# Top-32 attention and a squared-ReLU layer on one core: last score columns in a bank of their own, and identity products in TensorE's free places

## The chip, the core and the metric

The kernel runs on one core of one Trainium2 chip. Its engines are named as in the profile: PE (TensorE's products; PEld is its loading of weights), DVE (VectorE), ACT (ScalarE), POOL (GpSimd) and SP (SyncE, whose queue SPq starts transfers). The metric is the device time of one launch in microseconds (us); lower is better.

## What is computed

For each of 8 batches and 8 heads there are 576 queries, keys and values of 64 numbers. Of each query's 576 scores only those at or above its 32nd largest enter a softmax. The result, put together as 4608 rows of 512, goes through two matrix products with a squared ReLU between them.

```python
scores = scale * np.matmul(q, k.transpose(0, 1, 3, 2))          # (8, 8, 576, 576)
kth = np.partition(scores, -top_k, axis=-1)[..., -top_k:-top_k + 1]   # top_k = 32
scores = np.where(scores >= kth, scores, -1e9)
attn = np.exp(scores - np.max(scores, axis=-1, keepdims=True))
x = np.matmul(attn / (np.sum(attn, axis=-1, keepdims=True) + 1e-09), v)
...
h = x @ w_in                                # (4608, 512) x (512, 2048)
r = np.maximum(h, 0.0)
return (r * r) @ w_out                      # (2048, 512)
```

## The kernel before

**Unit of work.** A *pair* is 128 queries of two neighbouring heads (block 0 and block 1), 2 x 576 scores on 128 partitions. There are 144 pairs, 18 to a batch. The last 64 queries of four heads make a pair of another shape (`Z`), two to a batch.

**Steps of a pair.** PE makes the scores in three banks of PSUM (`scores`, tile `ps`, float32, 64 rows of the array for each head). ACT copies all 1152 columns to `s`. DVE and POOL find each row's 32nd largest value: an elementwise maximum `m` of the two halves of a row (DVE, which reads one half from PSUM and the other from `s`), a reduction `f` to quarters, sums and differences on POOL, and then MAX8 and MATCH_REPLACE8 in turns until `kth`. ACT makes a mask `w`; PE transposes `s` and adds the mask (`flip`: nine float32 transposes and nine bfloat16 products with `steep_bf`, in two parts of 4 and 5); ACT takes the exponential `p`; PE multiplies by the values (`vb`); ACT copies the result (`av`); DVE takes the reciprocal of the sums (`rzall`), POOL multiplies, PE transposes to `xt`. When a chunk of up to 512 rows is full, `feed` runs the layer: products with `win`, ReLU on ACT, squares, products with `wo`, and a store. This is called the layer below; a batch's layer runs while later pairs are in their attention.

**Buffers in PSUM.** The scores have one set of three banks, the transposed scores another (`ps_e`), and all else that PE writes takes turns in two single banks (`psum`).

**The scores before.** Block 0 lies at columns 0 to 575, block 1 at 576 to 1151. So block 0's last 64 columns share a bank with block 1's first 448, and the two heads use different rows of the array. They are written in two operations: the first makes block 0's 512 columns and all of block 1, the second makes block 0's last 64 and waits for the first by a semaphore; the order puts other work of PE between them where there is some.

**Order.** A planner lists every operation with an engine, an assumed duration, a priority and its inputs, plays the list through (`Plan.schedule`) and so fixes each engine's order, written out with semaphores. On the chip every engine follows that order strictly. `nbf` is the earliest time for an operation, and `lag` moves a chunk's layer to a lower priority.

Of the kernel before, what the change touches and what calls it, by code (L numbers as in the profile page):

```python
# [5 lines left out]
ALU = mybir.AluOpType  # L6
# [70 lines left out]
class Op:  # L77
    __slots__ = ("eng", "dur", "prio", "fn", "deps", "tiles", "takes", "n", "users", "start", "end",
                 "idx", "sem", "val", "ndma", "seq", "vc", "waits", "wars", "later", "nbf", "lk")
# [5 lines left out]
class Plan:  # L85
# [3 lines left out]
    def op(self, eng, dur, prio, fn, r=(), w=(), u=(), hold=(), take=(), after=(), order=(), sem=None, ndma=0, nbf=0.0, lk=False):  # L89

        o = Op()
        o.eng, o.dur, o.prio, o.fn = eng, dur - (.05 if eng == "act" else 0), prio, fn
        o.sem, o.ndma, o.seq, o.nbf, o.lk = sem, ndma, len(self.ops), nbf, lk
        o.takes = list(take)
        o.users = []
        o.start = o.end = o.idx = o.val = o.vc = None
        deps = set(after)
        for t in r:  # L100
            deps.update(t.writers)
        for t in u:
            deps.update(t.ops)
        for t in list(r) + list(w) + list(u) + list(hold):
            t.ops.append(o)
            t.left += 1
        for t in list(w) + list(u):
            t.writers.append(o)
        for t in o.takes:
            t.taker = o  # L110
        o.later = ({t.taker for t in list(r) + list(w) + list(u) + list(hold)} | set(order)) - deps - {o, None}
        o.deps = deps
        o.wars = list(w) + list(u)
        o.tiles = list(r) + list(w) + list(u) + list(hold)
        self.ops.append(o)
        return o

    def schedule(self, t0=0.0, latency=0.12, own=0.07):
# [24 lines left out]
        while events:  # L143
            t = events[0][0]
            while events and events[0][0] <= t + 1e-9:
                _, _, kind, x = heapq.heappop(events)
                if kind == "end":
                    done += 1
                    for tl in x.tiles:
                        tl.left -= 1  # L150
                        if tl.left == 0 and tl.slot is not None:
                            for i in range(tl.width):
                                tl.pool.last[tl.slot + i] = tl
                            tl.pool.give(tl.slot, tl.width)
                    for v in x.users:
                        left[v] -= 1
                        lat = (own if x.eng != "pe" else .25) if v.eng == x.eng else latency
                        readyat[v] = max(readyat[v], t + lat)
                        if left[v] == 0:
                            push(readyat[v], "ready", v)  # L160
                elif kind == "ready":
                    heapq.heappush(ready[x.eng], (x.prio, x.seq, x))
# [45 lines left out]
class Emitter:  # L208
# [59 lines left out]

    def emit(self, plan, e, eng):
        for o in plan.order[e]:  # L270
            for k, v in o.waits:
# [9 lines left out]
def bass_top_k_attn__then__act_relu_squared_kernel(  # L281
# [32 lines left out]
    STEP = 3.2  # L314

# [90 lines left out]

    def mm(o, l, r, start, stop=True):
# [5 lines left out]
    def build(full, weights, pl):  # L413
        state = {"n": 0, "u": 0, "last": {}}
# [6 lines left out]
        def load_pair(b, hp, base):  # L421
            rq, rk, rv = tile("rq"), tile("rk"), tile("rv")

            def load(t, src):
                def fn():
                    r = at(t)
                    res = [nc.sync.dma_start(r[:, 0:4, h, :], src[b, 2 * hp + h, 0:512, :].rearrange(
                        "(tb p) d -> p tb d", p=P)) for h in range(2)]
                    res.append(nc.sync.dma_start(
# [14 lines left out]
            pl.op("sp", 2.3, base - 79.9, load(rk, k), w=[rk], take=[rk], sem=slot_sem, ndma=3)  # L444
# [16 lines left out]
            o_q = pl.op("pe", .55, base - 45, t4(tq, rq), r=[rq], w=[tq], take=[tq, qk])  # L461
            pl.op("pe", .55, base - 44.9, t4(tk, rk), r=[rk], w=[tk], take=[tk], order=[o_q])
# [5 lines left out]
            pl.op("gp", .9, base + 5, lambda: gp.tensor_copy(at(vb)[:, :, 0:D], at(rv)[:, :, :]),  # L468
# [3 lines left out]
        def top_k(gi, qks, tg):  # L472
# [10 lines left out]
            def scores(part):  # L483
# [7 lines left out]
            def scores_z(part):  # L491
                o = wide(ss)
                for i, to, c0, n_, first in PIECES[part]:
                    x = at(qks[i])
                    for h in range(2):
                        ins = mm(o[64 * h:64 * h + 64, to:to + n_], x[64 * h:64 * h + 64, 0, 512:576],
                                 x[64 * h:64 * h + 64, 1, c0:c0 + n_], first)
                return ins

            fs = scores if gi != Z else scores_z  # L500
            qu = sorted(set(qks), key=lambda t: t.num)
            o_s = pl.op("pe", 1.2, tg - LEAD, lambda: fs(0), r=qu, w=[ss], take=[ss, st])
            pl.op("pe", .15, tg - LEAD, lambda: fs(1), r=qu, w=[ss], after=[o_s])
            cp = pl.op("act", 1.15, tg - LEAD + 1, lambda: act.copy(  # L504
                at(st)[:, :, :].rearrange("p i c -> p (i c)"), wide(ss)), r=[ss], w=[st])
# [44 lines left out]
            else:  # L550
# [3 lines left out]
                def whole(dur, prio, op, o, x, y, **kw):  # L554
# [3 lines left out]
                dve(.7, lambda: vec.tensor_tensor(  # L558
                    at(m)[:, :, :], wide(ss).rearrange("p (i c) -> p i c", i=2)[:, :, 0:HALF],
                    at(st)[:, :, HALF:S], ALU.max), dp=-ME, r=[ss], hold=[st], after=[cp], w=[m], take=[m])  # L560
                whole(1.45, tg, ALU.add, lambda: at(t1)[:, :, :], lambda: at(st)[:, :, 0:HALF],
# [4 lines left out]
                whole(.87, tg - MP, ALU.add, lambda: at(t2)[:, :, :], lambda: at(m)[:, :, 0:QUART],  # L566
                      lambda: at(m)[:, :, QUART:HALF], r=[m], w=[t2], take=[t2])
                mid = whole(.87, tg - MP, ALU.subtract, lambda: at(f)[:, :, QUART:HALF], lambda: at(t2)[:, :, :],
                            lambda: at(f)[:, :, 0:QUART], r=[t2], hold=[f], after=[big])
                low = whole(1.45, tg + 2, ALU.subtract, lambda: at(f)[:, :, HALF:S], lambda: at(t1)[:, :, :],  # L570
# [38 lines left out]
        def attend(gi, st, wt, tt):  # L609
# [14 lines left out]
            o_t = pl.op("pe", .75, tt, lambda: flip([0, 128, 256, 384], 0), r=[st, wt], w=[e], take=[e, pt])  # L624
            pl.op("pe", .95, tt + .1, lambda: flip([640, 768, 896, 1024, 512], 4), r=[st, wt], w=[e], order=[o_t])
# [4 lines left out]
        def collect(gi, groups, parts, hp, tt):  # L630
# [19 lines left out]
            pl.op("pe", .2 * nu, tt + 2, lambda: [fav(j, pt, vbs) for j, (pt, vbs) in enumerate(groups)][-1],  # L650
# [3 lines left out]
            rz = pl.op("dve", .1, tt + 4, lambda: vec.reciprocal(rzall[:, r0:r0 + nu], at(avs)[:, 0:nu, 64]), r=[avs])  # L654
            rzs.append(rz)
            pl.op("gp", .15 + .13 * nu, tt + 4, lambda: gp.tensor_tensor(  # L656
# [29 lines left out]
        def feed(chunk, xt, tm, step):  # L686
# [5 lines left out]
            lag = 0 if last else LAG  # L692
            gs = [tile("g") for _ in range(NFB // kf)]
            for i, g in enumerate(gs):
# [15 lines left out]
                ho = pl.op("pe", kf * 4 * (nt / 2200 + .01), tf + lag, fh, r=[xt], w=[hh], take=[hh, g], after=weights,  # L710
# [11 lines left out]
            for tb in range((nt + 127) // 128):  # L722
# [3 lines left out]
                for sub in range(4):  # L726
# [6 lines left out]
                    pl.op("pe", 1.0, to + lag + step * sub, fo,  # L733
# [57 lines left out]
    def setup(pl):  # L791
# [22 lines left out]
        for i in range(16):  # L814
# [6 lines left out]
            else:  # L821
# [7 lines left out]
                                 r=[s]))  # L829
        return [i1], pre, zeros, weights  # L830
# [26 lines left out]
    for o in main.ops[n_pre:]:  # L857
        if o.eng == "sp":
# [14 lines left out]
    with nc.Block() as blk:  # L873
        def emit(e, eng):
            em.emit(main, e, eng)
# [58 lines left out]
```

## Time and profile before

| | us |
|---|---|
| median of three runs (from 967.36 to 971.03) | 969.63 |
| the profiled execution | 972.14 |
| its span, from first to last instruction | 970.3 |
| PE, DVE, ACT, POOL busy | 887.8, 863.3, 737.5, 750.4 |

The span is 1.84 us shorter than the profiled execution's own time, and that execution is 2.5 us longer than the median. Busy times of PE count overlapping products once.

### The profile page before, as it was taken

The numbers are of one execution on the slowest core, as the hardware profiler recorded it, in microseconds if no ns is written. First come the engines' busy times: TensorE is split into PE (matmuls) and PEld (weight loads), VectorE is DVE, ScalarE is ACT, GpSimd is POOL, SyncE is SP. The second block draws the span as 40 slices with busy tenths as digits, with TensorE's granted clock in tenths as the row PEclk, the third lists the DMA queues.
The fourth block names the chain that finished last, engine by engine and source line by source line (L and its number), as shares of the span: only waits on it lengthen the run. The fifth ranks groups of instructions, "written<-read, shape, count | busy, mean of one in ns | idle before, by whom it ended". The sixth has DMA issues, their size and how long they took to land.

```text
span 970.3 us, 21522 instructions
## 1 busy us (share of the span) xinstructions
PE 887.8 (91%) x7650; PEld 620.2 (64%) x7650; DVE 863.3 (89%) x3269; ACT 737.5 (76%) x1133; POOL 750.4 (77%) x794
## 2 busy tenths in 40 slices
PE   5877789999799999999998999999999999999995
PEld 3655566777566666666766676666676655666654
DVE  1888799999999999999999999999999999786831
ACT  2555588898789877997789977998788879686752
POOL 5787688788877777778777787778799986599950
PEclk9976799999999999999999999999999999999998
DMA  6541153102310022001221112111111210000011
GB/s 155 143 124 67 44 136 79 38 15 60 87 38 15 20 67 71 16 15 38 59 49 39 39 35 74 25 39 38 36 48 26 53 33 23 23 11 13 22 34 37
DMA packets 126981, 48.15 MB, mean 50 GB/s; under 512 B 119184, under 2 KB 119184, under 8 KB 126864
## 3 DMA queue, kind: packets, MB, share of 16 engines
q1 hardware_dynamic: 126864, 46.69, 18.9%
q8 instruction: 62, 1.02, 0.4%
q14 instruction: 55, 0.45, 0.2%
HBM read 37.22 MB, written 9.44 MB: 48 GB/s over the span
## 4 chain that ended last, share of the span: by engine, by line
PE 44%; DVE 30%; POOL 10%; ACT 8%; issue 6%; DMA 0%; SPq 0%; POOLq 0%; DVEq 0%
PE ps L408 34%; PE ps L411 10%; DVE f L582 8%; DVE c L578 7%; DVE kth L585 6%; POOL f L555 6%; DVE m L558 5%; POOL t L555 3%; DVE f L563 3%; ACT p L626 3%; ACT s L504 2%; ACT w L593 1%; ACT g L706 1%; POOL x L656 1%; DMA rk<-in_k_dram 0%
## 5 line engine op out<-in xcount | busy, mean ns | idle before, releaser
L408 PE MATMUL ps<-qk 64*128 64x512 f32 (+6 forms) x1600 | 281.7, 413 | 30.0 <-DVE m L558 28.3
L408 PEld LDWEIGHTS ps<-qk 64*128 64x128 f32 (+1 forms) x1600 | 178.3, 183 | 141.6 <-DVE m L558 46.5
L582 DVE MATCH_REPLACE8 f<-c,f 128x104 f32<-128x104 f32 (+2 forms) x864 | 268.7, 320 | 0.0
L578 DVE MAX8 c<-f 128x8 f32<-128x104 f32 (+2 forms) x864 | 248.5, 325 | 0.2
L593 ACT ACTIVATE w<-s,kth 128x576 bf16<-128x576 f32 x288 | 220.6, 780 | 16.8 <-DVE kth L585 16.3
L555 POOL TENSOR_TENSOR t<-s 128x576 int32<-128x576 int32 x144 | 201.6, 1411 | 25.2 <-ACT s L504 25.1
L411 PE MATMUL ps<-ident,s 128*128 128x128 f32 x1296 | 204.1, 286 | 6.8 <-ACT w L593 6.3
L504 ACT COPY s<-ps 128x1152 f32<-128x1152 f32 x144 | 161.4, 1121 | 64.1 <-PE ps L408 62.8
L585 DVE MAX8 kth<-f 128x8 f32<-128x576 f32 x288 | 205.1, 751 | 2.4 <-POOL f L555 2.4
L555 POOL TENSOR_TENSOR f<-t,m 128x576 int32<-128x576 int32 x144 | 202.8, 1408 | 0.0
L626 ACT ACTIVATE p<-ps 128x1152 bf16<-128x1152 f32 x144 | 162.9, 1131 | 35.1 <-PE ps L408 34.3
L555 POOL TENSOR_TENSOR f<-t,f 128x288 int32<-128x288 int32 x144 | 114.5, 795 | 85.2 <-DVE f L563 82.6
L411 PEld LDWEIGHTS ps<-ident,s 128*128 128x128 f32 x1296 | 146.4, 144 | 35.5 <-ACT w L593 8.5
L558 DVE TENSOR_TENSOR m<-ps,s 128x576 f32<-128x576 f32 x144 | 107.9, 749 | 45.2 <-ACT s L504 41.9
L408 PE MATMUL ps<-wo,g 128*128 128x512 bf16 x576 | 143.4, 380 | 1.0 <-ACT xt L681 0.4
L408 PE MATMUL ps<-xt,win 128*128 128x512 bf16 (+3 forms) x704 | 134.3, 331 | 4.7 <-ACT xt L680 3.3
L408 PE MATMUL ps<-steep_bf,w 128*128 128x128 bf16 x1296 | 122.5, 223 | 0.0
L555 POOL TENSOR_TENSOR t<-m 128x288 int32<-128x288 int32 x144 | 115.0, 799 | 4.3 <-DVE m L558 4.3
L563 DVE TENSOR_REDUCE f<-m 128x288 f32<-128x576 f32 x144 | 106.4, 752 | 0.2
L706 ACT ACTIVATE g<-ps 128x512 bf16<-128x512 f32 (+1 forms) x152 | 85.3, 576 | 24.4 <-PE ps L408 23.8
L408 PEld LDWEIGHTS ps<-steep_bf,w 128*128 128x128 bf16 x1296 | 99.0, 100 | 3.9
L656 POOL TENSOR_TENSOR x<-av,rzall 128x256 bf16<-128x256 f32 (+1 forms) x88 | 47.1, 535 | 58.6 <-DVE rzall L654 58.2
(56 smaller groups left out, 750.7 us busy)
## 6 DMA issues: line engine op xcount, KB each, us to landing
rq<-in_q_dram SPq DMA_DIRECT2D x64, 128.0 KB, 2.5
rk<-in_k_dram SPq DMA_DIRECT2D x64, 128.0 KB, 2.6
rv<-in_v_dram SPq DMA_DIRECT2D x64, 128.0 KB, 2.4
out_dram<-o SPq DMA_DIRECT2D x31, 256.0 KB, 2.1
g<-in_moe_w_in_dram SPq DMA_DIRECT2D x8, 512.0 KB, 4.5
g<-in_moe_w_out_dram SPq DMA_DIRECT2D x8, 512.0 KB, 4.5
rv<-in_v_dram SPq DMA_DIRECT2D x96, 16.0 KB, 2.2
out_dram<-o SPq DMA_DIRECT2D x10, 128.0 KB, 2.3
```

Of the source, the lines that this page charges most:

```text
L408: return pe.matmul(o, l, r, start=start, stop=stop, skip_group_check=True)
L411: return pe.matmul(o, i, ident, is_transpose=True, skip_group_check=True, **kw)
L504: cp = pl.op("act", 1.15, tg - LEAD + 1, lambda: act.copy(at(st)[:, :, :].rearrange("p i c -> p (i c)"), wide(ss)), r=[ss], w=[st])
L555: return pl.op("gp", dur, prio, lambda: gp.tensor_tensor(o().bitcast(I32), x().bitcast(I32), y().bitcast(I32), op), **kw)
L558: dve(.7, lambda: vec.tensor_tensor(at(m)[:, :, :], wide(ss).rearrange("p (i c) -> p i c", i=2)[:, :, 0:HALF], at(st)[:, :, HALF:S], ALU.m ...
L563: big = dve(.67, lambda: vec.tensor_reduce(at(f)[:, :, 0:QUART], at(m)[:, :, :].rearrange("p i (a c) -> p i c a", a=2), AX.X, ALU.max), dp ...
L578: lambda i=i, t=t, c0=c0, c1=c1: vec.max(eighth(t, i), at(f)[:, i, c0:c1]),
L582: lambda i=i, t=t, c0=c0, c1=c1: vec.match_replace(at(f)[:, i, c0:c1], eighth(t, i), at(f)[:, i, c0:c1], NEG), hold=[f])]
L585: ks.append(chain(kth, i, prev[i] + [low], .665, lambda i=i: vec.max(eighth(kth, i), at(f)[:, i, :]), hold=[f]))
L593: pl.op("act", .77, tw + .8 * i, lambda i=i: act.activation(at(wt)[:, i, :], at(st)[:, i, :], ACTF.Relu, bias=kth[:, i, n:n + 1], scale=-1.0),
L626: pl.op("act", 1.15, tt + 1, lambda: act.activation(at(pt)[:, :, :].rearrange("p k q -> p (k q)"), wide(e), ACTF.Exp, scale=0.125), r=[e], ...
L706: return act.activation(at(g)[:, 0:kf * nt], bank(hh)[:, 0:kf * nt], ACTF.Relu)
```

## The change

**Scores.** Block 0's first 512 columns take the first bank, block 1's the second, and both blocks' last 64 the third. One operation makes all: block 0's 64, its 512, block 1's 512, then block 1's 64; before this last piece PE waits for a semaphore `fence` that block 0's 64 raise. ACT copies in two operations, the 1024 columns of the first two banks and the 128 of the third; `s` keeps its layout. For block 1 the maximum `m` reads the other half from PSUM than before.

**Identity products.** 133 operations of two products each (identity by identity, 512 columns, bfloat16) are added with the lowest priority, from time 0.45 i on in the planner's clock; each takes one of the two single banks of `psum`. Nothing reads them.

**Start.** Only the loads of values still wait for POOL's zeroing of `rv`; before, all loads did. The first load of k is issued from ACT's queue.

**Planner.** Assumed durations are lowered. A reciprocal counts as ready 1.5 us later than its input (`late`). The layer of the last batch's chunks, all but the very last, is given a lag of 10 where it had 0.

```diff
+            via = "act" if not full and not state["pairs"] else None
+            state["pairs"] += 1
+            pl.op("sp", 2.3, base - 79.9, load(rk, k, nc.scalar if via else nc.sync), w=[rk], take=[rk], sem=slot_sem,
+                  ndma=3, via=via)
...
-            PIECES = [[(0, 0, 0, 512, True), (1, 576, 512, 64, True), (1, 640, 0, 384, False), (1, 1024, 384, 128, True)],
-                      [(0, 512, 512, 64, False)]]
+            def scores():
                 o = wide(ss)
-                for h, to, c0, n_, first in PIECES[part]:
+                for h, to, c0, n_ in ((0, 1024, 512, 64), (0, 0, 0, 512), (1, 512, 0, 512), (1, 1088, 512, 64)):
                     x = at(qks[h])
+                    if to == 1088:
+                        pe.wait_ge(fence, fences[0])
                     ins = mm(o[:, to:to + n_], x[64 * h:64 * h + 64, 0, 128 * gi:128 * gi + 128],
-                             x[64 * h:64 * h + 64, 1, c0:c0 + n_], first)
+                             x[64 * h:64 * h + 64, 1, c0:c0 + n_], to != 1088)
+                    if to == 1024:
+                        fences[0] += 1
+                        ins.then_inc(fence, 1)
...
-            o_s = pl.op("pe", 1.2, tg - LEAD, lambda: fs(0), r=qu, w=[ss], take=[ss, st])
-            pl.op("pe", .15, tg - LEAD, lambda: fs(1), r=qu, w=[ss], after=[o_s])
-            cp = pl.op("act", 1.15, tg - LEAD + 1, lambda: act.copy(
-                at(st)[:, :, :].rearrange("p i c -> p (i c)"), wide(ss)), r=[ss], w=[st])
+            pl.op("pe", 1.25 if gi != Z else 1.4, tg - LEAD, scores if gi != Z else scores_z, r=qu, w=[ss], take=[ss, st])
+            cp = [pl.op("act", 1.1, tg - LEAD + 1, lambda: act.copy(
+                two(flat(), 640, 512), two(wide(ss), 512, 512)), r=[ss], w=[st]),
+                pl.op("act", .35, tg - LEAD + 1, lambda: act.copy(
+                    flat()[:, 512:640], wide(ss)[:, 1024:1152]), r=[ss], w=[st])]
...
-            lag = 0 if last else LAG
+            lag = 0 if end else LAGL if last else LAG
...
+        for i in range(int(WARM / .45)):
+            t = Tile(psum)
+            def warm(t=t):
+                for _ in range(2):
+                    ins = mm(bank(t), ident_bf[:, :], ident_bf[:, :].unsqueeze(1).broadcast_to([P, 4, P]), True)
+                return ins
+            pl.op("pe", .45, 1e5, warm, w=[t], take=[t], after=[i2], nbf=.45 * i)
...
-        if o.eng == "sp":
+        if o.eng == "sp" and o.takes and o.takes[0].pool.name == "rv":
             o.deps.update(zeros)
```

PE's order at the start of the program, before (`ident,rq` and `ident,rk` are transposes of loaded q and k, `qk` products are scores):

```order
L411 MATMUL ps<-ident,rq 128x128 x4
L411 MATMUL ps<-ident,rk 128x128 x4
L411 MATMUL ps<-ident,rq 128x64
L411 MATMUL ps<-ident,rk 128x64
L408 MATMUL ps<-qk 128x512
L408 MATMUL ps<-qk 128x64
L408 MATMUL ps<-qk 128x384
L408 MATMUL ps<-qk 128x128
L408 MATMUL ps<-qk 128x64
```

and with the change:

```order
L428 MATMUL ps<-ident_bf 128x512 x12
L431 MATMUL ps<-ident,rq 128x128 x4
L428 MATMUL ps<-ident_bf 128x512 x6
L431 MATMUL ps<-ident,rk 128x128 x4
L431 MATMUL ps<-ident,rq 128x64
L431 MATMUL ps<-ident,rk 128x64
L428 MATMUL ps<-ident_bf 128x512 x2
L428 MATMUL ps<-qk 128x64
L428 MATMUL ps<-qk 128x512 x2
L428 MATMUL ps<-qk 128x64
L428 MATMUL ps<-ident_bf 128x512 x10
```

Identity products (`ident_bf 128x512`) now stand between the steps. In all 266 are in the order, 44 of them ahead of the first pair's `flip`, 184 ahead of the 18th's end, and the last ahead of the 72nd's.

PE's order in the later first batches, before, between a `flip` in two parts and the layer's products (`xt,win`):

```order
L408 MATMUL ps<-qk 128x512
L408 MATMUL ps<-qk 128x64
L408 MATMUL ps<-qk 128x384
L408 MATMUL ps<-qk 128x128
L411 MATMUL ps<-ident,s 128x128 x5
L408 MATMUL ps<-steep_bf,w 128x128 x5
L408 MATMUL ps<-qk 128x64
L408 MATMUL ps<-xt,win 128x256 x16
```

and with the change, at the like place:

```order
L428 MATMUL ps<-qk 128x64
L428 MATMUL ps<-qk 128x512 x2
L428 MATMUL ps<-qk 128x64
L431 MATMUL ps<-ident,s 128x128 x5
L428 MATMUL ps<-steep_bf,w 128x128 x5
L428 MATMUL ps<-wo,g 128x512 x12
```

Block 0's last 64 columns, which stood apart behind a part of a `flip`, are now the first of four score products in a row.

SP's order at the start, before:

```order
L826 DMA g<-in_moe_w_in_dram 128x1024 x2
L427 DMA rq<-in_q_dram 128x4x64 x2
L429 DMA rq<-in_q_dram 64x2x64
L427 DMA rk<-in_k_dram 128x4x64 x2
L429 DMA rk<-in_k_dram 64x2x64
L436 DMA rv<-in_v_dram 128x4x64 x2
L440 DMA rv<-in_v_dram 64x64 x3
```

and with the change:

```order
L447 DMA rq<-in_q_dram 128x4x64 x2
L449 DMA rq<-in_q_dram 64x2x64
L456 DMA rv<-in_v_dram 128x4x64 x2
L460 DMA rv<-in_v_dram 64x64 x3
L447 DMA rq<-in_q_dram 128x4x64 x2
L449 DMA rq<-in_q_dram 64x2x64
```

The loads of weights stand behind the first four pairs' loads now, and the first k is gone from this queue (it is ACT's first).

## Rows read from the trace of the kernel before

**Rows 1.** The page: span, busy time by engine, TensorE's granted clock in 40 slices

```profile
span 970.3 us, 21522 instructions
...
PE 887.8 (91%) x7650; PEld 620.2 (64%) x7650; DVE 863.3 (89%) x3269; ACT 737.5 (76%) x1133; POOL 750.4 (77%) x794
...
PEclk9976799999999999999999999999999999999998
```

**Rows 2.** Windows: stretch, length, busy PE, PEld, DVE, ACT, POOL (instructions), clock, DMA

```profile
0.00:15.86 15.86, 6.88 (x24) 4.53 (x24) 0.00 (x0) 3.77 (x6) 7.18 (x33) 1.00 0.76 177
15.86:160.00 144.14, 114.91 (x880) 87.08 (x881) 121.51 (x453) 85.27 (x124) 113.95 (x114) 0.87 0.39 102
160.00:748.75 588.75, 558.67 (x5032) 394.70 (x5030) 580.96 (x2215) 495.15 (x753) 472.64 (x481) 1.00 0.17 42
748.75:963.20 214.45, 207.35 (x1720) 133.89 (x1718) 160.78 (x605) 152.72 (x252) 156.57 (x168) 0.99 0.10 27
```

**Rows 3.** One line's instructions up to 154 and up to 748.75 us: the `flip` products

```profile
L408 PE MATMUL ps<-steep_bf,w x162: 218/220/315, 32.6 to 153.6; 128*128 128x128 bf16 x162
...
L408 PE MATMUL ps<-steep_bf,w x1053: 218/220/315, 32.6 to 748.6; 128*128 128x128 bf16 x176
```

**Rows 4.** Waits between 15.86 and 160 us: in total, times, longest

```profile
DVE m L558 <- ACT s L504: 35.5, 10, 15.9
ACT s L504 <- PE ps L408: 29.8, 10, 4.2
```

**Rows 5.** Windows again (columns as in Rows 2): two stretches of lowered clock

```profile
52.00:64.00 12.00, 10.31 (x64) 7.85 (x64) 9.71 (x37) 4.67 (x7) 8.68 (x9) 0.57 0.51 140
...
80.00:104.00 24.00, 19.76 (x104) 15.33 (x104) 17.74 (x68) 8.62 (x12) 15.34 (x15) 0.51 0.13 44
```

**Rows 6.** Timeline of the start: start, length, engine, what, idle before it

```profile
4.75 1.66 SPq L429 DMA_DIRECT2D rk<-in_k_dram  x1
...
8.06 1.12 PE L411 MATMUL ps<-ident,rq 128*128 128x128 f32 x4 [8.06 <-DMA rq<-in_q_dram]
...
9.46 1.11 PE L411 MATMUL ps<-ident,rk 128*128 128x128 f32 x4 [0.28 <-DMA rk<-in_k_dram]
...
15.86 0.76 DVE L558 TENSOR_TENSOR m<-ps,s 128x576 f32<-128x576 f32 x1 [15.86 <-ACT s L504]
...
31.66 1.11 PE L411 MATMUL ps<-ident,s 128*128 128x128 f32 x4
...
37.49 0.66 PE L411 MATMUL ps<-ident,rk 128*128 128x128 f32 x4
```

**Rows 7.** Timeline of PE at full clock: scores, and what follows them

```profile
69.15 1.36 PE L408 MATMUL ps<-qk 64*128 64x512 f32 x8
70.44 0.77 PE L411 MATMUL ps<-ident,s 128*128 128x128 f32 x5
...
76.61 0.43 PE L408 MATMUL ps<-qk 64*128 64x64 f32 x2
76.97 0.29 PE L411 MATMUL ps<-ident_bf,x 128*128 128x128 bf16 x2
```

**Rows 8.** Timeline of PE: products under way from 69.3 to 69.5, and from 69.66 to 69.72

```profile
69.15 0.82 PE L408 MATMUL ps<-qk 64*128 64x512 f32 x4
...
69.15 1.12 PE L408 MATMUL ps<-qk 64*128 64x512 f32 x3
```

**Rows 9.** Groups by form, PE, 748.75 to 970.3 us, and the timeline's last products

```profile
L408 PE MATMUL ps<-wo,g 128*128 128x512 bf16 x256 | 62.6, 380 | 0.6 <-ACT xt L681 0.4 <-ACT av L652 0.2
...
959.51 3.62 PE L408 MATMUL ps<-wo,g 128*128 128x512 bf16 x16
```

**Rows 10.** Groups by form of the whole trace: ACT's copies out of PSUM

```profile
L504 ACT COPY s<-ps 128x1152 f32<-128x1152 f32 x144 | 161.4, 1121 | 64.1 <-PE ps L408 62.8
...
L464 ACT COPY qk<-ps 128x512 f32<-128x512 f32 x32 | 18.7, 588 | 13.4 <-PE ps L411 13.3
L466 ACT COPY qk<-ps 128x128 f32<-128x128 f32 x32 | 8.8, 274 | 0.1
```

More of the change, by code (lines that the diff above doesn't have):

```diff
@@ L78 @@
     __slots__ = ("eng", "dur", "prio", "fn", "deps", "tiles", "takes", "n", "users", "start", "end",
-                 "idx", "sem", "val", "ndma", "seq", "vc", "waits", "wars", "later", "nbf", "lk")
+                 "idx", "sem", "val", "ndma", "seq", "vc", "waits", "wars", "later", "nbf", "lk", "late",
+                 "via")
 ENGS = ("pe", "act", "dve", "gp", "sp")
@@ L87, in __init__, with op @@
         self.ops = []
-    def op(self, eng, dur, prio, fn, r=(), w=(), u=(), hold=(), take=(), after=(), order=(), sem=None, ndma=0, nbf=0.0, lk=False):
+    def op(self, eng, dur, prio, fn, r=(), w=(), u=(), hold=(), take=(), after=(), order=(), sem=None, ndma=0, nbf=0.0, lk=False, late=0.0, via=None):
         o = Op()
-        o.eng, o.dur, o.prio, o.fn = eng, dur - (.05 if eng == "act" else 0), prio, fn
-        o.sem, o.ndma, o.seq, o.nbf, o.lk = sem, ndma, len(self.ops), nbf, lk
+        o.eng, o.dur, o.prio, o.fn = eng, dur - (.1 if eng == "act" else 0), prio, fn
+        o.sem, o.ndma, o.seq, o.nbf, o.lk, o.late, o.via = sem, ndma, len(self.ops), nbf, lk, late, via
         o.takes = list(take)
@@ L267, in sem, with via @@
         return self.dma[k[1]][0] if isinstance(k, tuple) else self.sems[k]
+    def via(self, plan, e):
+        for o in plan.order["sp"]:
+            if o.via == e:
+                assert not o.waits
+                for i in o.fn():
+                    i.then_inc(self.sem(o.idx[0]), 16)
     def emit(self, plan, e, eng):
         for o in plan.order[e]:
+            if o.via is not None:
+                continue
             for k, v in o.waits:
@@ L405, in bass_top_k_attn__then__act_relu_squared_kernel, with two @@
     CHUNKS += [[(NB - 1, 0, 128)], [(NB - 1, 128, 128)]]
+    def two(ap, step, n_):
+        return bass.AP(ap.tensor, ap.offset, [ap.ap[0], [step, 2], [1, n_]])
+    fence, fences = nc.alloc_semaphore("fence"), [0]
     def mm(o, l, r, start, stop=True):
@@ L413, in build @@
     def build(full, weights, pl):
-        state = {"n": 0, "u": 0, "last": {}}
+        state = {"n": 0, "u": 0, "pairs": 0, "last": {}}
         kths, rzs = [], []
@@ L556, in whole @@
                         o().bitcast(I32), x().bitcast(I32), y().bitcast(I32), op), **kw)
[L558 to L561, printed above, removed]
+                dve(.67, lambda: vec.tensor_tensor(
+                    at(m)[:, :, :], two(wide(ss), 736, HALF), two(flat()[:, HALF:], HALF, HALF), ALU.max),
+                    dp=-ME, r=[ss], hold=[st], after=cp, w=[m], take=[m])
+                whole(1.38, tg, ALU.add, lambda: at(t1)[:, :, :], lambda: at(st)[:, :, 0:HALF],
                       lambda: at(st)[:, :, HALF:S], r=[st], w=[t1], take=[t1])
@@ L621, in flip @@
                 return ins
[L624 to L625 removed]
+            o_t = pl.op("pe", .68, tt, lambda: flip([0, 128, 256, 384], 0), r=[st, wt], w=[e], take=[e, pt])
+            pl.op("pe", .84, tt + .1, lambda: flip([640, 768, 896, 1024, 512], 4), r=[st, wt], w=[e], order=[o_t])
             pl.op("act", 1.15, tt + 1, lambda: act.activation(
@@ L709, in feed @@
                 w_ = kf * nt
-                ho = pl.op("pe", kf * 4 * (nt / 2200 + .01), tf + lag, fh, r=[xt], w=[hh], take=[hh, g], after=weights,
+                ho = pl.op("pe", .03 + kf * 4 * (nt / 2340 + .002), tf + lag, fh, r=[xt], w=[hh], take=[hh, g], after=weights,
                       nbf=tf if not last else 0)
```

48 lines of the change are left out of this document (26 added, 22 removed).

## The prediction

> **What bounds the kernel now.** I read the page first, then the busy time of each engine stretch by stretch, then the waits inside the stretches that lose time.
>
> The page [rows 1] shows two engines near the span: PE at 91% and DVE at 89%. A share of the whole span says little when the limit changes, so the windows [rows 2] are the view to trust. Four stretches stand out. Up to 15.86 us DVE has nothing to do. From there to 160 us DVE is busy 121.5 of 144.1 us, so it loses 22.6. From 160 to 748.75 us it is busy 581.0 of 588.8 us: DVE bounds this stretch, and it loses only 7.8. From 748.75 to 963.2 us PE is busy 207.4 of 214.5 us while DVE is at 160.8: PE bounds the end. Then 7.1 us remain for the last copy and store.
>
> The cuts at 153.6 and 748.6 us are chosen by progress: 162 `flip` products have been issued by the first and 1053 by the second [rows 3], nine to a pair, so 18 and 117 of the 144 pairs. The 99 pairs between take 595 us, 6.0 us each. That is DVE's pace, and PE's work per pair fits in it.
>
> Why does DVE lose 22.6 us early? The waits between 15.86 and 160 us [rows 4] say that `m` waits for the copy of the scores and the copy for the score products on PE (35.5 us with the 15.9 of the start, so 19.6 us, over nine waits). PE is late there because it is slow. The granted clock reads 0.57 and 0.51 in two stretches that together hold 36 us, [rows 5], against 1.00 from 160 us on [rows 2]; 0.5 is the 1.2 GHz level. The column reads 1.00 before 15.86 us too, but there and at 31.66 us four transposes take 1.1 us, and at 37.49 us 0.66 [rows 6]: until about 36 us the products also ran at the halved level, whatever the column says.
>
> **The first 160 us.** The identity products are to keep PE busy, and so its clock up. They cost PE time: 16 products of 512 columns took 3.62 us, start to start 0.216 each [rows 9]. 184 of them stand ahead of the 18th pair's end, so 184 x 0.216 = 40 us. All the rest of PE's work up to 160 us was 6.9 + 114.9 = 121.8 us busy [rows 2]. About 55 of these lay at the halved clock: 30.1 us in the two stretches of [rows 5], and an estimated 25 in the first 36 us. By transposes at both levels, 1.1 against 0.66 us for four [rows 6], these 55 us shrink to about 32, so about 98 us remain. With the identity products that is 138 us of PE's work. DVE's work for the same content is 121.5 us after a start at about 14 us, so 136. PE is thus filled to the brim, but the content that took 160 us fits in 138 if nothing waits, and in 160 if the identity products only replace the pauses. An order followed strictly on one engine with no spare room will wait somewhere; I take 7 us for that and 145 us in all: **-15 us**, between -23 (DVE's 136 with a little waiting) and 0.
>
> The start itself is inside this. The weights' two loads and then k on SP's queue keep k's last transfer from being issued until 6.4 us, and its transposes wait until 9.46 [rows 6]. With q first and k on another queue, both issues should end near 2.5 us and, with the same 3 us from issue to use, be there at 5.6. But 12 identity products at the halved clock, 0.43 us each, stand ahead of the transposes from about 2 us on and end near 7, and 6 more stand between q and k. So of the 6.4 us from k's transposes to `m`, some is paid back: DVE's first `m` moves from 15.86 to 14 at best guess, 13 to 16.6 as bounds.
>
> **From pair 18 to pair 117.** DVE's work is not changed: the same nine kinds of operation with the same sizes. ACT pays for two copies in place of one. 1152 columns took 1.121 us, 128 take 0.274, 512 take 0.588 [rows 10]; from the first two 1024 columns cost 1.121 - 128 x 0.83 ns = 1.015, so 1.29 in place of 1.12, 24 us over 144 pairs. ACT is busy 495 of 588.8 us here [rows 2] and would be at 512: covered. If that cover were gone, `m` would come 0.17 us later per pair, as it needs both copies; against that the scores end earlier, since their second part no longer stands behind other work of PE. PE has room. So **0 us**, and I keep -5 (two thirds of DVE's lost 7.8) and +5 (ACT's other copies, which the new order often sets between the two) as bounds.
>
> **The last 27 pairs, where PE is the bound.** The score products cost, start to start, 70.44 - 69.15 = 1.29 us for the first part and 76.97 - 76.61 = 0.36 for the second [rows 7], 1.65 in all. In the first part the two heads overlap: four products are under way at once, and later three [rows 8]. One head had 512 columns in it and the other 576; now both have 576. If the overlap stays, the longer head sets the time as before, 1.29 us, and the second part is gone: 0.36 us a pair. The wait for `fence` stands behind 1024 columns that follow the product it waits for, so it should be over when PE comes to it; queued behind it are the last 64 columns and the next transposes, and ACT's copy waits for these. Price of the overlap lost: below, as a rival.
>
> In this stretch stand 20 pairs of the plain shape, so 20 x 0.36 = 7.2 us, and three of the Z shape, to which I give 0.27 each by its smaller products (an estimate between 0 and 0.36), 0.8. The layer's work hardly moves: after the 117th `flip` the order counts 252 products with `wo` for 256 [rows 9], 124 of 512 columns with `win` for 128, and none of 384 for 4: 8 x 0.216 + 4 x 0.16 = 2.4 us less. Sixteen transposes of loaded q and k, at 0.12 us by [rows 7], were moved ahead of the cut: 1.9 us. Sum **-12 us**, between -18 (DVE's work of 160.8 us and a chain of some 30 after it allow not much more) and 0. The new lag only reorders the layer against the attention inside this stretch; as long as PE has no pauses the sum does not change. The reciprocal's delay removes some of DVE's waiting, which is not the bound here.
>
> **Sum.** 970.3 - 15 + 0 - 12 = 943.3 us of span; with the 1.84 us around it 945.1; the profiled execution was 2.5 us above the median, so 942.6, rounded to 943 us.
>
> **A rule that speaks against the score's price.** The overlap of the heads is read from [rows 8] and from the eight products' 1.36 us. The Trainium skill, "TensorE: Matmul & The Clock Gate", Part 3, under "What overlaps and what doesn't", says that matmuls start and end strictly in program order. By that rule block 1's products could not pass block 0's second half, and with block 0's 64 and 512 in front the heads would overlap only where they meet. In this trace the products of a score do overlap, but it doesn't show for certain which head each belongs to.
>
> **Rivals.**
> - *The heads run one behind the other.* Block 0's 576 columns go first and block 1's start only with their second half. Taking 1.29 us for 576 columns of a head in two passes, a pass is 0.64, so a pair would cost 3 x 0.64 = 1.9 us, 0.25 more than before. The last stretch then gains nothing (-4.3 from the moved work, +5.8), and PE at 95% from 160 to 748.75 us [rows 2] would come to 99%, about 5 us of waiting. Time 970.3 - 15 + 5 + 1.5, as a median 961. For it: the order of the pieces. Against: [rows 8].
> - *The identity products only fill PE.* They stand in PE's strict order whether PE is late or not, so PE never catches up; the content of the first 160 us takes 160 again, and only the last stretch gains: 970.3 - 12, as a median 957. For it: 138 of 145 us are work. Against: 19.6 us of waits had the halved clock as their cause.
> - *DVE alone bounds the end.* The early gain is the full 23, the middle gains 5, the last stretch 18: 924, as a median 923.
> - *Slower: identity products at the halved clock.* If the clock stays halved until the sixth pair, 102 identity products cost 22 us more and that third of PE's other work 21 more: 180 us for the content of the first 160, which with -12 ends at 978, as a median 977. It decides against the change from about 27 us of such excess on, so if the clock is not up by the fourth pair. Against it: the clock came up by 36 us even with PE's pauses of the start, and now PE has work from 2 us on.
>
> **How the numbers follow.** The forecast has 0.60 and its own range is 932 to 953; identity products that only fill PE 0.15; the end bounded by DVE 0.10; heads in a row 0.08; slower 0.06; nothing of this 0.01. A difference of 0.5% (5 us) is about what measurement can tell from none. Faster than 964.8: the forecast, the third rival, and most of the first two, 0.87; within 5 us 0.06; slower 0.07. For the range I leave out the slow rival above and the far end of the third below: 925 to 963, which takes in the bounds 0 of either large term with the other kept.
>
> **What would show it.** The granted clock should be near full from about 10 us on, and `flip` of pair 18 should end near 139 us rather than 153.6. Four score products in a row should take about 1.29 us to the next product. DVE should stay at 99% from pair 18 to 117, and 27 pairs at the end should take about 202 us with PE without pauses. I am wrong if DVE still loses 20 us early, if a pair's score takes 1.6 us or more, or if DVE's share in the middle falls below 97% with `m` waiting for ACT's second copy.

## The result and the profile after

The changed kernel takes 934.18 us (median of four runs, 933.6 to 936.56) against 970.33 for the kernel before beside it: a ratio of 0.9637 (0.9609 to 0.9665), 36 us less. The profiled execution took 934.26 us with a span of 932.1.

The page, as in [rows 1]:

```profile
span 932.1 us, 21508 instructions
...
PE 857.0 (92%) x7513; PEld 579.9 (62%) x7596; DVE 864.8 (93%) x3269; ACT 744.3 (80%) x1277; POOL 750.9 (81%) x794
...
PEclk9999999999999999999999999999999999999998
```

The granted clock reads 9, which is 90% or more, from the first slice on, and DVE does about the same 865 us of work (863.3 before) in a shorter span. The windows, cut at about the same progress as in [rows 2]:

```profile
0.00:13.00 13.00, 10.47 (x45) 4.90 (x46) 0.14 (x1) 3.80 (x6) 5.20 (x32) 1.00 0.68 137
13.00:145.00 132.00, 126.14 (x1065) 82.90 (x1064) 125.66 (x471) 95.11 (x160) 118.85 (x119) 1.00 0.45 118
145.00:726.75 581.75, 530.04 (x4800) 369.75 (x4856) 579.75 (x2193) 495.93 (x846) 471.43 (x478) 1.00 0.18 45
726.75:925.00 198.25, 190.31 (x1609) 122.31 (x1634) 159.23 (x607) 149.24 (x266) 155.43 (x168) 1.00 0.08 23
```

From 13 to 145 us PE is busy 126 of 132 us and DVE loses only 6.3 us; before, DVE lost 22.6 of 144. The middle is DVE's as before. In the last stretch PE is busy 190.3 us for 207.4 before (16 of 252 products with `wo` and 9 of 124 of 512 columns with `win` have no record in this trace, so it may be up to 25 x 0.216 = 5.4 us more).

Progress can be counted on PE, by `flip` as in [rows 3], or on DVE, by the MAX8 that gives `kth`, twice to a pair. One line's instructions up to the 18th and up to the 117th pair, in the kernel after (the last two numbers of the first part are first and last start):

```profile
L428 PE MATMUL ps<-steep_bf,w x162: 219/219/219, 25.2 to 138.3; 128*128 128x128 bf16 x162
...
L428 PE MATMUL ps<-steep_bf,w x1053: 219/219/311, 25.2 to 726.5; 128*128 128x128 bf16 x176
...
L616 DVE MAX8 kth<-f x36: 726/746/757, 20.8 to 126.9; 128x8 f32<-128x576 f32 x36
...
L616 DVE MAX8 kth<-f x234: 726/748/786, 20.8 to 720.6; 128x8 f32<-128x576 f32 x117
```

and DVE's in the kernel before:

```profile
L585 DVE MAX8 kth<-f x36: 733/750/767, 25.8 to 147.4; 128x8 f32<-128x576 f32 x36
...
L585 DVE MAX8 kth<-f x234: 731/751/780, 25.8 to 742.3; 128x8 f32<-128x576 f32 x117
```

With about 0.75 us for the last MAX8, the end of each stretch and the change of each length are:

| us | before | after | change |
|---|---|---|---|
| 18th `kth` ends | 148.2 | 127.6 | -20.6 |
| from there to the 117th `kth` | 594.8 | 593.8 | -1.0 |
| from there to the end of the span | 227.3 | 210.7 | -16.6 |

By `flip` the same three read -15.3, -6.8 and -16.1. The middle did not get faster: `flip` of the 18th pair ended 5.6 us behind `kth` before (153.8 against 148.2) and 10.9 after (138.5 against 127.6), and PE catches this up later. Where DVE is the bound, progress is read on DVE.

The start and one score of the middle, in PE's and DVE's timeline (columns as in [rows 6]):

```profile
2.06 4.56 PE L428 MATMUL ps<-ident_bf 128*128 128x512 bf16 x12 [2.06 <-POOL ident_bf L826]
...
6.46 0.60 PE L431 MATMUL ps<-ident,rq 128*128 128x128 f32 x4
...
8.42 0.60 PE L431 MATMUL ps<-ident,rk 128*128 128x128 f32 x4
...
12.86 0.76 DVE L589 TENSOR_TENSOR m<-ps,s 128x576 f32<-128x576 f32 x1 [12.86 <-ACT s L535]
...
603.26 1.35 PE L428 MATMUL ps<-qk 64*128 64x64 f32 x8 [0.77 <-DVE m L589]
604.53 0.25 PE L431 MATMUL ps<-ident_bf,x 64*64 64x64 bf16 x4
```

The first transposes take 0.60 us, where before they took 1.12 [rows 6]: the clock was up already at 6.5 us. DVE's first `m` starts at 12.86 instead of 15.86. A whole score takes 604.53 - 603.26 = 1.27 us to the next product, against 1.29 for the first part alone before [rows 7]: the heads still overlap. Each product of a score stands in the trace twice. Of this score's eight records, these have started from 603.26 to 603.41 us (groups by form):

```profile
L428 PE MATMUL ps<-qk 64*128 64x512 f32 x1 | 0.7, 693 | 0.0
L428 PE MATMUL ps<-qk 64*128 64x64 f32 x1 | 0.3, 320 | 0.8 <-DVE m L589 0.8
```

A product of 512 columns has started while block 0's 64 columns, first in the order, have only the first of their two records.

The wait that cost 19.6 us before (beside the start's own 15.9, [rows 4]), here from 17 us to the 18th `kth`:

```profile
DVE m L589 <- ACT s L535: 2.1, 6, 0.5
```

So the forecast's numbers came true, with both large terms a few us short by DVE's progress. Whether its causes did, the profile of two kernels cannot say: four edits act on the same first 160 us. The experiments take them apart.

### The profile page after: what moved, and what is told of

The parts are those of the page before. It is cut to its first block, busy times and chain, and to the rows that moved or that the text cites. A ratio compares the mean times of both kernels' runs of the same rounds, so it can differ in the third digit from the quotient of the medians.

```text
span 932.1 us, 21508 instructions
## 1 busy us (share of the span) xinstructions
PE 857.0 (92%) x7513; PEld 579.9 (62%) x7596; DVE 864.8 (93%) x3269; ACT 744.3 (80%) x1277; POOL 750.9 (81%) x794
## 3 DMA queue, kind: packets, MB, share of 16 engines
q1 hardware_dynamic: 125664, 46.39, 19.6%
## 4 chain that ended last, share of the span: by engine, by line
DVE 49%; PE 38%; ACT 9%; issue 3%; POOL 1%; POOLq 0%
PE ps L428 30%; DVE f L613 14%; DVE kth L616 11%; DVE c L609 11%; PE ps L431 8%; DVE m L589 6%; DVE f L594 6%; ACT p L657 2%; ACT s L533 2%; ACT w L624 1%; ACT g L737 1%; ACT g L751 1%; ACT qk L488 1%; DVE rzall L685 0%; ACT o L768 0%
## 5 line engine op out<-in xcount | busy, mean ns | idle before, releaser
L609 DVE MAX8 c<-f 128x8 f32<-128x104 f32 (+2 forms) x864 | 245.0, 323 | 0.1
L428 PE MATMUL ps<-qk 64*128 64x64 f32 (+3 forms) x1280 | 207.8, 443 | 26.8 <-DVE m L589 26.4
L533 ACT COPY s<-ps 128x1024 f32<-128x1024 f32 x144 | 146.5, 1017 | 78.2 <-PE ps L428 77.7
L431 PE MATMUL ps<-ident,s 128*128 128x128 f32 x1296 | 196.2, 279 | 3.4 <-ACT w L624 2.7
L428 PEld LDWEIGHTS ps<-qk 64*128 64x128 f32 (+1 forms) x1280 | 126.0, 176 | 106.7 <-issue 41.5
L428 PE MATMUL ps<-wo,g 128*128 128x512 bf16 x528 | 133.8, 379 | 3.6 <-issue 0.8
L428 PE MATMUL ps<-xt,win 128*128 128x512 bf16 (+3 forms) x669 | 125.9, 323 | 11.8 <-ACT g L737 4.9
L589 DVE TENSOR_TENSOR m<-ps,s 128x576 f32<-128x576 f32 x144 | 107.9, 749 | 23.1 <-ACT s L535 17.2
L428 PE MATMUL ps<-steep_bf,w 128*128 128x128 bf16 x1296 | 119.5, 219 | 0.0
L428 PEld LDWEIGHTS ps<-steep_bf,w 128*128 128x128 bf16 x1296 | 96.8, 98 | 3.3
L428 PEld LDWEIGHTS ps<-xt,win 128*128 128x128 bf16 x704 | 58.0, 98 | 49.8 <-ACT g L737 9.4
```

The costliest lines, as they stand in the source:

```text
L428: return pe.matmul(o, l, r, start=start, stop=stop, skip_group_check=True)
L431: return pe.matmul(o, i, ident, is_transpose=True, skip_group_check=True, **kw)
L533: cp = [pl.op("act", 1.1, tg - LEAD + 1, lambda: act.copy(two(flat(), 640, 512), two(wide(ss), 512, 512)), r=[ss], w=[st]), pl.op("act", . ...
L589: dve(.67, lambda: vec.tensor_tensor(at(m)[:, :, :], two(wide(ss), 736, HALF), two(flat()[:, HALF:], HALF, HALF), ALU.max), dp=-ME, r=[ss] ...
L609: lambda i=i, t=t, c0=c0, c1=c1: vec.max(eighth(t, i), at(f)[:, i, c0:c1]),
```

## The experiments

Ratios are to the kernel before, run on the same chip. The two runs with identity products of another size keep the order of every engine; for every other edit the planner orders the rest anew, so that these runs show the edit together with the order that comes of it.

| run | median us | ratio (95%) | 18th `kth` ends |
|---|---|---|---|
| before | 970.3 | | 148.2 |
| after | 934.18 | 0.9637 (0.9609 to 0.9665) | 127.6 |
| no identity products | 929.98 | 0.9566 (0.9532 to 0.9599) | 127.3 |
| identity products of 32 columns | 932.39 | 0.9605 (0.9582 to 0.9627) | 125.9 |
| three identity products in place of two | 959.86 | 0.9886 (0.9863 to 0.9909) | 147.1 |
| before, with identity products only | 971.77 | 1.0017 (0.9995 to 1.004) | 132.7 |
| before, with the new scores only | 948.56 | 0.9806 (0.9756 to 0.9856) | 131.8 |
| after, with the scores of before | 968.0 | 0.9994 (0.9973 to 1.0015) | 134.0 |
| after, with the planner's numbers of before | 940.01 | 0.9708 (0.9663 to 0.9753) | 124.6 |
| after, with the start of before | 937.48 | 0.9681 (0.9637 to 0.9726) | 130.6 |
| after, again | 934.67 | 0.9638 (0.9617 to 0.9659) | 127.9 |
| no identity products, again | 931.69 | 0.9613 (0.9582 to 0.9644) | 128.2 |
| before, both parts of a score joined | 962.23 | 0.9919 (0.99 to 0.9939) | 136.3 |
| after, with the scores of before and no identity products | 991.38 | 1.0229 (1.0205 to 1.0253) | 154.8 |

### No identity products

```diff
-    WARM = 60
+    WARM = 0
```

> The changed kernel without the identity products; the planner orders the rest anew. Theory A (the early gain of 20.6 us, by the time of the 18th pair's kth, comes from PE's clock): the clock falls to half in stretches between 50 and 110 us as before, the 18th pair's kth comes at about 140 us in place of 127.6, and the median is 943 to 950. Rival B (it comes from the earlier start and the tighter order): the kth stays near 128 to 130 us and the median is 931 to 936.

It was faster than the change, not slower. Windows of this kernel (columns as in [rows 2]), the first 18 pairs' `kth`, and DVE's wait for the scores' copy up to there:

```profile
13.00:145.00 132.00, 101.78 (x907) 77.29 (x909) 125.23 (x474) 93.60 (x159) 119.02 (x121) 0.94 0.45 117
...
64.00:96.00 32.00, 21.67 (x178) 16.79 (x176) 30.56 (x121) 18.77 (x29) 29.05 (x30) 0.84 0.25 77
```

```profile
L616 DVE MAX8 kth<-f x36: 730/748/762, 21.2 to 126.6; 128x8 f32<-128x576 f32 x36
```

```profile
DVE m L589 <- ACT s L535: 4.0, 4, 1.4
```

PE is busy 24 us less in 13 to 145 us, its clock falls at times (0.84 from 64 to 96 us), and yet the 18th `kth` ends as early as with the identity products: DVE waits 4.0 us instead of 2.1. Here the lowered clock costs nothing, since PE hardly comes late for DVE. Run again later beside the change itself, it took 931.69 us, and the change 934.67:

> The changed kernel without the identity products, a second time and beside the changed one. If the products only take PE's time (theory E), 928 to 932 and below the changed kernel by 3 us or more; if the first result was a chance, within 2 us of it.

> The changed kernel itself, beside the kernel without identity products on one chip: 933 to 936.

The two intervals, 0.9613 (0.9582 to 0.9644) and 0.9638 (0.9617 to 0.9659), overlap; those of the first runs, 0.9566 (0.9532 to 0.9599) and 0.9637 (0.9609 to 0.9665), do not, but these two stem from separate sets of runs. The identity products bring nothing to the whole change; whether they cost up to 0.7% is not settled.

### Identity products of another size

Same order, less or more work in it:

```diff
-                    ins = mm(bank(t), ident_bf[:, :], ident_bf[:, :].unsqueeze(1).broadcast_to([P, 4, P]), True)
+                    ins = mm(bank(t)[:, 0:32], ident_bf[:, :], ident_bf[:, 0:32], True)
```

> The changed kernel with the order of every engine kept, but each identity product 32 columns wide in place of 512, so that PE pauses where they stand. Theory A: the clock is granted in part only, DVE waits for scores again, median 940 to 950. Rival B (order): 930 to 934, since PE has 35 us less to do in the first 120 us.

```diff
-                for _ in range(2):
+                for _ in range(3):
```

> The changed kernel with the same order, but three products in each identity operation in place of two: 133 x 0.216 = 29 us more work for PE, 20 us of it ahead of the 18th pair's end. If PE is filled to the brim there, as the prediction worked out (138 us of work in 145), the 18th kth comes 12 to 20 us later and the median is 944 to 954. Rival: PE still has pauses that take them in, 934 to 938.

The thin ones give 932.39 us, and their interval overlaps those of the change and of the kernel without identity products. The third product adds 133 x 0.216 = 29 us to PE's work, 20 of them ahead of the 18th pair's end, and the time grows by 25.7, more than was expected. One window of this kernel, and its wait from 12 to 158 us:

```profile
13.00:158.00 145.00, 139.69 (x1098) 88.96 (x1094) 120.21 (x445) 91.22 (x153) 112.79 (x113) 1.00 0.38 105
```

```profile
DVE m L589 <- ACT s L535: 27.3, 12, 15.0
```

The 18th `kth` comes at 147.1, nearly where it was before the change, at full clock. So the change left PE no room in this stretch: the forecast's "filled to the brim" holds, and of the 20 us more work up to there 19.5 are paid.

### Identity products alone

The loop of the change's diff that adds the 133 operations was put into the kernel before, and nothing else.

> The kernel before with the identity products added and nothing else changed. Theory A: early clock near 1.0, the 18th kth 10 to 18 us earlier than 148.2, median 951 to 960. Rival B: no gain, 966 to 972, because the old scores leave PE less room and the identity products only stand in its way.

The time is that of the kernel before, 971.77 us. But the gain is there, and is lost again. The first 18 pairs of this kernel:

```profile
L585 DVE MAX8 kth<-f x36: 740/749/759, 23.7 to 131.9; 128x8 f32<-128x576 f32 x36
```

and its end, in the timeline (the kernel before issued its last store at 963.77 us):

```profile
948.73 13.78 PE L408 MATMUL ps<-ident_bf 128*128 128x512 bf16 x62
949.54 0.34 SPq L745 DMA_DIRECT2D out_dram<-o  x1
...
962.67 0.15 DVE L858 TENSOR_REDUCE flag<-ps 1x1 int32<-1x3 f32 x1 [17.23 <-PE ps L856]
```

The last store is issued 14.2 us earlier than before. Then 62 identity products, for which this order had found no place earlier, take 13.78 us of PE, and the closing test, a small product that DVE's `flag` waits for, stands behind them. What has the lowest priority is not dropped: it comes last, and here the end of the program waits for it. (One of the ten executions took 1760.88 us at full clock. The program makes all pairs a second time when the closing test asks for it, which may have happened there; no trace of that execution was kept, and why is open.)

### New scores alone

The scores' hunks of the change's diff, with `two` and `fence`, were put into the kernel before.

> The kernel before with the new scores alone (third bank, one operation, two copies), nothing else changed. Theory C (the score products carry the gain early and late, since each pair frees 0.36 us of PE and no second part stands behind other work): median 934 to 946, the 18th kth some 10 us or more earlier. Rival D (the planner's new numbers and the start carry it): 955 to 968.

948.56 us, 21 less than before and a little above what was expected. One window, and the `kth` of the first 18 and the first 117 pairs of this kernel:

```profile
13.00:136.80 123.80, 92.19 (x795) 70.25 (x792) 114.11 (x429) 83.42 (x140) 107.23 (x107) 0.90 0.48 121
```

```profile
L599 DVE MAX8 kth<-f x36: 742/752/773, 24.2 to 131.1; 128x8 f32<-128x576 f32 x36
...
L599 DVE MAX8 kth<-f x234: 727/752/780, 24.2 to 719.8; 128x8 f32<-128x576 f32 x117
```

The 18th `kth` comes 16.4 us earlier than before, with the clock still lowered (0.90) and no identity product. So the scores shorten the first 160 us too, by as much as the identity products alone do (15.5). The 117th comes 22.5 us earlier (720.5). From there to the end of the span (943.8) are 223.3 us, only 4.0 less than before.

### The scores of before in the changed kernel, with and without identity products

The reverse edit, then also `WARM = 0`:

```diff
+            o_s = pl.op("pe", 1.2, tg - LEAD, lambda: fs(0), r=qu, w=[ss], take=[ss, st])
+            pl.op("pe", .15, tg - LEAD, lambda: fs(1), r=qu, w=[ss], after=[o_s])
...
-            pl.op("pe", 1.25 if gi != Z else 1.4, tg - LEAD, scores if gi != Z else scores_z, r=qu, w=[ss], take=[ss, st])
```

> The changed kernel, identity products, start and planner's numbers included, with the scores of before. Theory C: 958 to 972, near the kernel before. Rival D: 938 to 946.

> The changed kernel with the scores of before and without identity products: the start and the planner's numbers alone. If the identity products cost most where PE is the bound (theory E), it is clearly below the 968.0 of the same kernel with them, 948 to 960. If start and numbers gain only with the new scores, 964 to 970.

968.0 and 991.38 us; the second lies above both figures that were expected. With the two runs of the change that stand beside them this makes a square:

| | identity products | none |
|---|---|---|
| new scores | 934.2, 934.7 | 930.0, 931.7 |
| scores of before | 968.0 | 991.4 |

With the scores of before the identity products are worth 23 us, with the new ones nothing. The kernel with neither, its page, first window (columns as in [rows 2]), `kth` of 117 pairs, and DVE's wait from 154.8 to 761.4 us:

```profile
PEclk9986779999999999999999999999999999999999
```

```profile
15.86:160.00 144.14, 115.46 (x814) 88.01 (x812) 112.53 (x423) 80.80 (x117) 106.02 (x106) 0.81 0.40 105
```

```profile
L608 DVE MAX8 kth<-f x234: 730/754/774, 22.5 to 760.6; 128x8 f32<-128x576 f32 x117
```

```profile
DVE m L581 <- ACT s L527: 10.2, 16, 2.9
```

Here the clock is at 0.81, lower than the 0.87 of [rows 2], DVE is busy 112.5 us instead of 121.5, and the 18th `kth` comes at 154.8, later than before. With the old scores, the planner's numbers and the start of the change alone make the kernel 2.3% slower. By DVE's progress 6.6 us of that are in the first 18 pairs and 11.8 between the 18th and the 117th (606.6 us for 594.8), where `m` waits 10.2 us for the scores' copy and before waited 2.9; the last stretch takes as long as before (226.9 for 227.3).

### Both parts of a score joined

The layout of before, but both parts in one operation, with a semaphore between them, so that no other work of PE comes between:

```diff
-            o_s = pl.op("pe", 1.2, tg - LEAD, lambda: fs(0), r=qu, w=[ss], take=[ss, st])
-            pl.op("pe", .15, tg - LEAD, lambda: fs(1), r=qu, w=[ss], after=[o_s])
+            def joined():
+                fences[0] += 1
+                fs(0).then_inc(fence, 1)
+                pe.wait_ge(fence, fences[0])
+                return fs(1)
+            pl.op("pe", 1.6, tg - LEAD, joined, r=qu, w=[ss], take=[ss, st])
```

> The kernel before with its old layout, but both parts of a score in one operation, the second part behind a semaphore wait for the first: no other work of PE between them, and no bank of its own. If the gain of the new scores is that nothing stands between the parts, the median is near that of the new scores alone, 946 to 954. If it is PE's time, which is not saved here (the wait idles PE for some 0.3 us more), 968 to 980.

A score and what follows it, in this kernel's timeline, and the `kth` of its first 18 and first 117 pairs:

```profile
609.05 1.85 PE L410 MATMUL ps<-qk 64*128 64x512 f32 x10
610.83 0.25 PE L413 MATMUL ps<-ident_bf,x 64*64 64x64 bf16 x4
```

```profile
L592 DVE MAX8 kth<-f x36: 742/759/792, 27.7 to 135.5; 128x8 f32<-128x576 f32 x36
...
L592 DVE MAX8 kth<-f x234: 742/773/804, 27.7 to 725.1; 128x8 f32<-128x576 f32 x117
```

The score costs PE 1.78 us, 0.13 more than the two parts before, and still the kernel is 8.7 us faster, between the two figures that were expected, with the 18th `kth` 11.8 us earlier. ACT's copy needs both parts; before, the second stood behind other work of PE. So the new scores' gain of 21 has two parts. About 9 us are had with the old layout and more work of PE, when nothing stands between the parts. The other 12 or so come with the bank of their own, which saves PE 1.78 - 1.27 = 0.51 us a score: 20 scores of the last stretch make 10 us. The stages agree. The joined kernel is 17.2 us ahead of before at the 117th `kth` (725.8 for 743.0), and loses 6.3 of it where PE is the bound: 233.6 us to the end of the span for 227.3, and for 223.3 with the new scores alone.

### The planner's numbers and the start

All durations of the diff go back to those of before, `LATE` and `LAGL` to 0; the core of it:

```diff
-        o.eng, o.dur, o.prio, o.fn = eng, dur - (.1 if eng == "act" else 0), prio, fn
+        o.eng, o.dur, o.prio, o.fn = eng, dur - (.05 if eng == "act" else 0), prio, fn
...
-    LATE = 1.5
-    LAGL = 10
+    LATE = 0.0
+    LAGL = 0
```

> The changed kernel with the planner's durations of before, and no delay of reciprocals nor lag of the last layer. Theory C: within 8 us of the changed kernel, 930 to 942. Rival D: 945 to 965.

940.01 us, 5.8 more than the change, with intervals that just touch. The end of this kernel's timeline, against 925.20 us for the change's last store, and the `kth` of its first 117 pairs:

```profile
925.54 6.44 PE L428 MATMUL ps<-ident_bf 128*128 128x512 bf16 x28
926.35 0.34 SPq L776 DMA_DIRECT2D out_dram<-o  x1
...
931.91 0.19 PE L888 MATMUL ps<-fone 128*1 128x3 f32 x2
```

```profile
L616 DVE MAX8 kth<-f x234: 729/751/772, 20.6 to 710.5; 128x8 f32<-128x576 f32 x117
```

Again identity products are left over, 28 of them for 6.44 us, ahead of the closing test. The last store itself is only 1.2 us later. From it to the end of the span 11.1 us pass, against 6.9 in the change, so some 4 of the 5.8 us are these leftovers; no run removed them alone. Otherwise the new numbers move time about: with the old ones the 117th `kth` comes 10.2 us earlier (711.2 for 721.4), and from there to the last store it takes 11.3 us more (215.1 for 203.8). The old order leaves more of PE's work for the end, among it 24 products of the chunk `xz` with `win` and 40 transposes of q and k, where the new one leaves none and 16.

Then the start: the first load of k goes through SP's queue again, and all loads wait for the zeroing.

```diff
-            via = "act" if not full and not state["pairs"] else None
+            via = None
...
-        if o.eng == "sp" and o.takes and o.takes[0].pool.name == "rv":
+        if o.eng == "sp":
```

> The changed kernel with the start of before (all loads wait for the zeroing of rv, the first k goes through SP's queue). DVE's first operation was 3.0 us earlier with the change (12.86 for 15.86). If DVE bounds all that follows, the median is 2 to 4 us above the changed kernel's, 936 to 938; if the 3 us are lost in waits later, it is 933 to 935.

DVE's first `m` in this kernel:

```profile
14.77 0.76 DVE L589 TENSOR_TENSOR m<-ps,s 128x576 f32<-128x576 f32 x1 [14.77 <-ACT s L535]
```

937.48 us, 3.3 more than the change, as was expected, but with overlapping intervals. The first `m` stands 1.9 us later than in the change, not 3.0 as between the kernels before and after, and the 18th `kth` 3.0 us later. So the new start seems to be worth some 2 to 3 us that reach the end; the runs don't separate it from the new order.

## Why the prediction came out as it did

The time lies 9 us below the forecast, inside its own range. Its steps, one by one:

- **The first 160 us, size.** By the forecast's own cut, `flip` of the 18th pair, -15.3 us came for -15, at 138.5 us where 139 was given. By DVE's progress it is -20.6, and the 7 us taken for waits were too many: `m` waits 2.1 us. PE is late, but with `flip`, not with the scores, and so the missing 5 us came back in the middle, where by `flip` the forecast's 0 ± 5 was passed.
- **The first 160 us, cause: this step failed.** The forecast read that 19.6 us of waits had the halved clock as their cause, gave the cure to the identity products, and counted the scores' 0.36 us a pair only in the last stretch. The runs showed two cures, each nearly enough: identity products alone 132.7, new scores alone 131.8 (at clock 0.90), both with the new start and numbers 127.6, and without the identity products again 127.3. What DVE waited for was a complete score; here a higher clock brought it sooner, and so did a score that is not in two parts with other work between them. The gains don't add, because DVE's own work is the floor under both: after the change it is busy 125.7 of the 132 us.
- **Filled to the brim.** Right: of the third product's 20 us up to the 18th `kth`, 19.5 were paid there (147.1 for 127.6).
- **The start.** `m` at 12.86 us where 14 was taken and 13 was the bound. The clock was up by 6.5 us, while the estimate took identity products at the halved level until near 7: the twelve took 4.40 us to the next product, 0.37 each, not 0.43.
- **The middle.** Right on DVE: -1.0. ACT's second copy stayed covered.
- **The score.** Right: 1.27 us against 1.29. So the rival of heads in a row falls, and its 1.9 us with it. The Trainium skill, "TensorE: Matmul & The Clock Gate", Part 3, "What overlaps and what doesn't", says that matmuls start and end strictly in program order. The starts up to 603.41 us, shown with the result, do not agree with that.
- **The last 27 pairs.** -16.6 for -12. By starts in the trace the scores gave 39.9 - 31.9 = 8.0, as the sum had it; transposes gave about 2.5 for 1.9, and the layer's part by the order 2.4. About 1 us is a short stretch of halved clock that the kernel before had at 954 us; the remaining 2.7 have no row of their own. But the size came out in part by luck. The new scores alone save the same 8 us of PE, by starts, but gain 4.0 us here: in their order 24 products of `xz` with `win` stand behind the 117th `kth`, where the kernel before had 8. Planner, start and identity products with the scores of before gain 3.6 (965.9 - 742.2 = 223.7 us) or, without identity products, 0.4; only together do they reach 16.6. The forecast let the new numbers reorder work inside this stretch; they also move PE's work out of it into the middle, as the run with the old numbers shows.
- **The other rivals.** "Only fill PE" (957) falls as a time, but its thought was half right: in the finished kernel the identity products replace pauses that no longer cost anything. "DVE alone bounds the end" (923) falls, PE is busy 190.3 of 198.25 us there. The slower one falls, the clock being up before the first score.

Of the 36 us the new scores alone bring 21. Without identity products, numbers and start bring some 18 to 20 more on top of them, but with the scores of before the same two cost 20. Left out of the whole change one at a time, numbers and start cost 5.8 and 3.3 us; how the rest divides between them was not separated. The lowest medians are those of the change without its identity products, 930.0 and 931.7 us in two sets of runs, the second not clear of the change beside it.

## What to carry to other kernels

A lowered clock matters where the slowed engine then comes late for the one that bounds the stretch; look for what makes the result late as a whole before paying for work that keeps the clock up. Two edits that cure the same wait don't add, so each has to be tried alone and left out alone, and left out it may prove to be worth nothing. Two others may be worth something only together. Filler, work that nothing reads, of lowest priority needs an end: what the order cannot place goes last, ahead of whatever closes the program.

## What the runs showed of the hardware that was not expected

- The clock came up sooner when PE had large products from the start: with 12 of them from 2.06 us on, the transposes at 6.46 us already take 0.60 us; without, transposes took 1.11 us as late as 31.66 [rows 6].
- The clock's column did not show the low level of the start in the kernel before (1.00 up to 15.86 us, [rows 2], beside transposes of 1.12 us). Durations of one kind of product at several places say more there.
- A wait on a semaphore between products on different rows of the array cost nothing visible when 1024 columns stood between signal and wait (1.27 us for the whole score). Where the signal comes from the product just ahead, as in the joined scores, the ending of 64 columns and the wait come to 1.78 - 1.29 = 0.49 us.
